# Second products of a fused attention and feed-forward block: parts of 256 and 320 columns instead of 288 and 288

## The chip, the core and the metric

The kernel runs on one core of a Trainium2 chip. The metric is the device time of one execution in microseconds (us). It was 1181.57 us before the change, the median of 3 runs from 1181.06 to 1181.97 us.

## What is computed

The input is x, 2048 rows of 576 numbers. Each row is normalised; from the normalised rows come two branches, and both are added to x:

```python
def _A_ref(x, wqkv, wo):                      # 32 heads of 18, W = 8, dil = 2
    qkv = (x @ wqkv).reshape(B, S, 3, H, Dh)...
    logits = einsum("bhsd,bhswd->bhsw", q, kg) * scale   # keys at s, s-2, ... s-14
    o = einsum("bhsw,bhswd->bhsd", softmax(masked logits), vg)
    return o @ wo
def _B_ref(x, w1, w2):                        # 576 -> 4608 -> 576
    return maximum(x @ w1, 0) @ w2
xn = _layernorm(x)
return x + _A_ref(xn, A_wqkv, A_wo) + _B_ref(xn, B_w1, B_w2)
```

All data are 32-bit floats.

## The kernel before

[...] A product is then the sum of three: high by high, high by low, low by high. The 576 rows of a contraction make four tiles of 128 and one of 64; with the 64-row rests packed in pairs, a product over 576 rows takes 14 matmuls (the list TERMS), and one over 128 rows takes three.

The 2048 rows are worked in two phases of 1024 (even and odd rows, so that the attention's step of two becomes a step of one). A phase has eight tiles of 128 rows, X[ph, i], which hold x first and collect all sums. The hidden width of 4608 is cut into 36 blocks of 128, twelve chunks (c) of three (f). The main loop runs over 288 slots: for each phase, chunk, block of 256 rows (tb, four of them) and f.

In a slot n the loop does, in this order, h_mm(n + 2), the tasks listed for the slot, and o_mm(n):

- h_mm makes the **first products**: 14 matmuls of 128 rows by 256 columns into one PSUM tile named ph. ScalarE writes the high part of the positive values (hhi, line 500), VectorE the rest (hlo, line 503).
- Tasks are the products with wqkv (14 matmuls of 432 columns into a tile named pm, in qkv_tile), loads and splits of weights, transposes, and wo_b. Attention itself runs on VectorE in a background queue that is drained according to two estimated clocks, t["pe"] and t["dve"]; mm() charges the first by the number of columns it is told.
- o_mm makes the **second products**. For each of the two 128-row tiles (k) there is a PSUM tile named po of two banks, 512 numbers a partition each. The stationary operand is a block of hhi or hlo, the moving one a half of a 128 x 576 block of w2 (w2t), high or low. For each of the three terms j there are two matmuls, h = 0 and h = 1, one for each half of 576 columns; each goes to the start of its own bank. So a slot has 12 such matmuls, in which the halves alternate. Sums are kept in PSUM over the three f of a chunk, and after f = 2 o_out adds them to X on VectorE (line 544, one instruction for both halves). There are two po tiles in all, one for each k.
- wo_b multiplies one tile of the attention's result by wo: 14 terms, two matmuls of 288 columns each, into two pm tiles, added to X by two instructions (line 466). This occurs 16 times.

The last slot is treated apart. Its matmuls are sorted by half, so that the first half is complete sooner, and each half is added (line 550) and sent to the output on its own (line 551), from two queues.

All matmuls but the transposes have line 105, the helper mm. TensorE loads the stationary operand anew for each matmul (PEld in the profile).

Of the kernel before, what the change touches and what calls it, by code (L numbers as in the profile page):

```python
# [10 lines left out]
F32 = mybir.dt.float32  # L11
F32R = mybir.dt.float32r
AF = mybir.ActivationFunctionType
ALU = mybir.AluOpType
# [3 lines left out]
P = 128  # L18
# [29 lines left out]
def tile_body(ctx: ExitStack, tc: tile.TileContext, x, wqkv, wo, w1, w2, out):  # L48
    nc = tc.nc
    S, D = x.shape  # L50
# [5 lines left out]
    KT = 4  # L56
    DR = D - KT * P
    D2 = D // 2
    scale = Dh ** -0.5
    SPC = NTB * C  # L60
    SPP = NCH * SPC
# [21 lines left out]
    ps_m = pool("ps_m", 2, space=PSUM)  # L83
# [15 lines left out]
    o_v = out.rearrange("(p i two) d -> two i p d", i=NI, two=NPH)  # L99
# [4 lines left out]
    def mm(o, l, r, start, stop, n):  # L104
        nc.tensor.matmul(o, l, r, start=start, stop=stop)  # L105
        t["pe"] += n / 2400.0 + 0.002

    def dve(n):
        t["dve"] += (n + 130) / 960.0
# [111 lines left out]
    X, XT, XN, MR = {}, {}, {}, {}  # L221
# [7 lines left out]
    def stats(ph, i, parts=False):  # L229
# [7 lines left out]
        def sums():  # L237
            for h in range(2):
                nc.vector.bn_stats(st[:, h, :], xt[:, h * D2 : (h + 1) * D2])  # L239

# [66 lines left out]
    TERMS = [(k, k) for k in range(KT)] + [(5 + k, k) for k in range(KT)] + [(4, 4)] + [(k, 5 + k) for k in range(5)]  # L307
# [149 lines left out]

    def wo_b(ph, i):
        d, w = OT.pop((ph, i)), WO[ph]
        po = [ps_m.tile([P, D2], F32, name="pm") for _ in range(2)]  # L460
        for j, (a, b) in enumerate(TERMS):
            for h in range(2):
                mm(po[h], d[a], w[b][:, h * D2 : (h + 1) * D2], j == 0, j == len(TERMS) - 1, D2)
        for h in range(2):
            acc = X[ph, i][:, h * D2 : (h + 1) * D2]
            nc.vector.tensor_tensor(acc, po[h], acc, op=ALU.add)
            dve(D2)

    left = {(ph, i): 2 for ph in range(NPH) for i in range(NI)}

    def done(ph, i):
        left[ph, i] -= 1
        if left[ph, i] == 0:
            nc.sync.dma_start(o_v[ph, i], X[ph, i])
# [3 lines left out]
    H, PO = {}, {}  # L478
# [14 lines left out]
    def h_out(n, parts=False):  # L493
        pt = HP.pop(n)
        hi = hp.tile([P, TBN], F32R, name="hhi")
        lo = hp.tile([P, TBN], F32R, name="hlo")
        H[n] = (hi, lo)

        def high():
            nc.scalar.activation(hi, pt, AF.Relu)  # L500

        def low():
            nc.vector.scalar_tensor_tensor(lo, pt, 0.0, f32(hi), op0=ALU.max, op1=ALU.subtract)  # L503
            t["dve"] = max(t["dve"], t["pe"] + 0.6)
            dve(TBN)

        if not parts:
            high()
            low()
        return high, low  # L510

    def h_mm(n):
        h_terms(n, TERMS)
        h_out(n)

    def o_mm(n, out=True):
        ph, c, tb, f = slots[n]
        hi, lo = H.pop(n)
        w = W2[ph, c, f]
        end = n == len(slots) - 1  # L520
        for k in range(2):
            if f == 0:
                PO[k] = ps_o.tile([P, 2, 512], F32, name="po")
            cs = slice(k * P, (k + 1) * P)
            terms = [(j, l, b, h) for j, (l, b) in enumerate(((hi, 0), (hi, 1), (lo, 0))) for h in range(2)]
            if end:
                terms.sort(key=lambda z: z[3])
            for j, l, b, h in terms:
                mm(
                    PO[k][:, h, 0:D2], l[:, cs], w[:, b, h * D2 : (h + 1) * D2],  # L530
                    f == 0 and j == 0, f == C - 1 and j == 2, D2,
                )
        if out:
            o_out(n)

    def o_out(n, which=range(2)):
        ph, c, tb, f = slots[n]
        if f < C - 1:
            return
        for k in which:  # L540
            i = 2 * tb + k
            acc = X[ph, i].rearrange("p (h c) -> p h c", h=2)
            if n < len(slots) - 1:
                nc.vector.tensor_tensor(acc, PO[k][:, :, 0:D2], acc, op=ALU.add)  # L544
                dve(D)
                if c == NCH - 1:
                    done(ph, i)
                continue
            for h in range(2):
                nc.vector.tensor_tensor(acc[:, h], PO[k][:, h, 0:D2], acc[:, h], op=ALU.add)  # L550
                (nc.scalar if h else nc.sync).dma_start(o_v[ph, i][:, h * D2 : (h + 1) * D2], acc[:, h])
            left[ph, i] -= 1
            assert left[ph, i] == 0

# [12 lines left out]
    for ph in range(NPH):  # L567
        b = ph * SPP
# [14 lines left out]
        for i in range(NI):  # L583
            z = s + WO_STEPS[i]
            late(z, wo_a, ph, i)
            at(z + 1, wo_f, ph, i)
            late(z + 2, wo_s, ph, i)
            at(z + 3, wo_b, ph, i)
            at(z + 3, done, ph, i)
# [63 lines left out]
    x2[1]()  # L653
    x2[3]()
    o_mm(0)
    o_mm(1)
    make_xt(0, 3, bank=ps_h)
    o_mm(2, out=False)
    stats(0, 4)
    stats(0, 5)  # L660
# [4 lines left out]
    h4 = h_out(4, parts=True)  # L665
    h4[0]()
    o_out(2, (0,))
    make_xt(0, 4)
    o_out(2, (1,))
    h4[1]()  # L670
    h_terms(5, TERMS)
# [47 lines left out]
```

## Time and profile before

| | us |
|---|---|
| Median of 3 runs (lowest, highest) | 1181.57 (1181.06, 1181.97) |
| The profiled execution | 1181.42 |
| Its span, from first to last instruction | 1179.7 |
| TensorE busy | 1171.0 |
| VectorE busy | 818.8 |
| ScalarE busy | 301.9 |

The span is what the profile sees of the execution; 1.7 us lie around it. TensorE's busy time is that of matmuls which overlap one another, so that a single one's duration is not its price. A row of the timeline has the start in us, the length in us, the engine, the line, the operation, the tiles written and read, the shape and the count of instructions merged into it; a row of the groups has the total busy time and the mean duration in ns of one instruction, and then the idle time before the group with what ended it.

### The profile page before, as it was taken

To read this page: it belongs to the slowest core of one execution; us is meant where nothing else is said; L and a number is where in the kernel's file an instruction comes from. 1 tells how busy PE (TensorE), PEld (TensorE's weight loads), DVE (VectorE), ACT (ScalarE), POOL (GpSimd) and SP (SyncE) were. 2 spreads that over 40 slices of the span, in tenths; PEclk is the share of its full clock that TensorE was granted. 3 is DMA by queue.
4 is the path that set the end of the run, shared out by engine and by line. 5 is a ranking of instruction groups with operands and counts; after the bars stand their busy time and mean duration, and the time that the engine had idled before them with its cause. 6 is when DMAs were issued, how large, how long until landed. Compare 5 with 4: busy or idle time off the path is not lost.

```text
span 1179.7 us, 21695 instructions
## 1 busy us (share of the span) xinstructions
PE 1171.0 (99%) x8936; PEld 1162.3 (99%) x8936; DVE 818.8 (69%) x1298; ACT 301.9 (26%) x738; POOL 47.5 (4%) x70
## 2 busy tenths in 40 slices
PE   8999999999999999999999999999999999999998
PEld 8999999999999999999999999999999999999998
DVE  7427875888687678877673288758777884887752
ACT  5412222131222222321233123121222322222210
POOL 3200000010000000000020000000100000000000
PEclk9999999999999999999999999999999999999999
DMA  5312121130321211355342113030302313113431
GB/s 182 97 34 76 55 61 56 38 108 1 99 58 46 74 48 42 94 129 134 107 148 66 46 53 88 27 83 23 96 22 79 79 34 89 54 30 99 110 99 61
DMA packets 137650, 86.15 MB, mean 73 GB/s; under 512 B 48864, under 2 KB 121312, under 8 KB 137552
## 3 DMA queue, kind: packets, MB, share of 16 engines
q1 hardware_dynamic: 134736, 76.28, 23.7%
q10 hardware_dynamic: 2816, 8.49, 2.5%
q8 instruction: 70, 1.15, 0.4%
q14 instruction: 28, 0.23, 0.1%
HBM read 66.58 MB, written 9.96 MB: 65 GB/s over the span
## 4 chain that ended last, share of the span: by engine, by line
PE 96%; DVE 1%; DMA 1%; ACT 0%; issue 0%; POOL 0%; SPq 0%; DVEq 0%; ACTq 0%; POOLq 0%
PE ph L105 38%; PE po L105 38%; PE pm L105 20%; PE pm L274 0%; DVE bst L239 0%; DMA xn<-turned 0%; DMA x<-in_x 0%; DMA st<-in_wqkv 0%; DMA turned<-tr 0%; DVE pr L395 0%; POOL rstd L245 0%; DVE w2t L141 0%; ACT xn L257 0%; DVE hlo L503 0%; DVE x L550 0%
## 5 line engine op out<-in xcount | busy, mean ns | idle before, releaser
L105 PE MATMUL ph<-xT,w1t 128*128 128x256 f32 x4018 | 509.3, 278 | 0.7 <-ACT xT L279 0.7
L105 PEld LDWEIGHTS ph<-xT,w1t 128*128 128x128 f32 x4018 | 489.1, 188 | 1.1 <-ACT xT L279 1.0
L105 PE MATMUL po<-w2t,hhi 128*128 128x288 f32 x2304 | 400.7, 296 | 0.0
L105 PEld LDWEIGHTS po<-w2t,hhi 128*128 128x128 f32 x2304 | 337.0, 188 | 1.0
L500 ACT ACTIVATE hhi<-ph 128x256 fp32r<-128x256 f32 x287 | 109.9, 383 | 583.4 <-PE ph L105 560.2
L105 PE MATMUL po<-w2t,hlo 128*128 128x288 f32 x1152 | 245.0, 293 | 0.0
L503 DVE SCALAR_TENSOR_TENSOR hlo<-ph,hhi 128x256 fp32r<-128x256 f32 x287 | 120.8, 421 | 169.2 <-ACT hhi L500 168.5
L544 DVE TENSOR_TENSOR x<-po,x 128x576 f32<-128x576 f32 x190 | 142.5, 756 | 67.2 <-PE po L105 64.1
L105 PE MATMUL pm<-wq,xT 128*128 128x432 f32 x896 | 185.5, 358 | 0.0
L105 PEld LDWEIGHTS po<-w2t,hlo 128*128 128x128 f32 x1152 | 183.8, 188 | 0.0
L105 PEld LDWEIGHTS pm<-wq,xT 128*128 128x128 f32 x896 | 163.8, 188 | 5.6
L358 DVE TENSOR_TENSOR pr<-qo,k 128x1152 f32<-128x1152 f32 x64 | 85.8, 1348 | 0.0
L361 DVE TENSOR_REDUCE lg<-pr 128x64 f32<-128x1152 f32 x64 | 84.9, 1342 | 0.0
L388 DVE TENSOR_TENSOR pr<-lg,v 128x1152 f32<-128x1152 f32 x64 | 84.6, 1348 | 0.2
L141 DVE TENSOR_TENSOR w2t<-st,w2t 128x576 fp32r<-128x576 f32 x72 | 54.3, 754 | 40.4 <-ACT w2t L137 40.2
L395 DVE TENSOR_TENSOR pr<-pr 128x288 f32<-128x288 f32 (+1 forms) x128 | 70.4, 598 | 0.1
L141 DVE TENSOR_TENSOR w1t<-st,w1t 128x640 fp32r<-128x640 f32 x70 | 57.3, 818 | 12.1 <-ACT w1t L137 12.0
L137 ACT ACTIVATE w2t<-st 128x576 fp32r<-128x576 f32 x72 | 49.3, 685 | 55.1 <-PE po L105 46.5
L327 ACT ACTIVATE k<-pm 128x144 f32<-128x144 f32 x64 | 18.6, 291 | 146.5 <-PE pm L105 146.5
L137 ACT ACTIVATE w1t<-st 128x640 fp32r<-128x640 f32 x72 | 52.9, 735 | 2.5 <-DMA st<-in_w 2.3
L364 POOL TENSOR_SCALAR_AFFINE_SELECT lg<-lg 1x512 f32<-1x512 f32 x8 | 9.4, 1172 | 836.7 <-DVE lg L361 836.7
L105 PE MATMUL pm<-wq,oT 128*128 128x288 f32 x224 | 35.2, 296 | 0.8 <-ACT oT L451 0.8
(71 smaller groups left out, 444.2 us busy)
## 6 DMA issues: line engine op xcount, KB each, us to landing
st<-in_w SPq DMA_DIRECT2D x72, 288.0 KB, 3.0
st<-in_w SPq DMA_DIRECT2D x72, 256.0 KB, 3.1
st<-in_wqkv SPq DMA_DIRECT2D x32, 216.0 KB, 3.1
turned<-tr SPq DMA_DIRECT2D x64, 80.0 KB, 2.2
xn<-turned SPq DMA_DIRECT2D x16, 320.0 KB, 3.3
st<-in_w SPq DMA_DIRECT2D x144, 32.0 KB, 2.8
x<-in_x SPq DMA_DIRECT2D x15, 288.0 KB, 4.4
out<-x SPq DMA_DIRECT2D x14, 288.0 KB, 2.2
```

Of the source, the lines that this page charges most:

```text
L105: nc.tensor.matmul(o, l, r, start=start, stop=stop)
L137: nc.scalar.activation(hi, src, AF.Copy)
L141: nc.vector.tensor_tensor(lo, src, f32(hi), op=ALU.subtract)
L327: nc.scalar.activation(k[:, W - 1 + i, :], pq[:, 1, :], AF.Copy)
L358: nc.vector.tensor_tensor(pr[i], q, window(k, i), op=ALU.mult)
L361: nc.vector.tensor_reduce(lg[:, i], pr.pop(i).rearrange(heads, d=Dh), axis=AX.X, op=ALU.add)
L364: nc.gpsimd.affine_select(out=z, in_=z, pattern=[[1, NI], [1, W], [0, HG]], compare_op=ALU.is_ge, fill=-1e9 / scale, base=1 - W, channel_m ...
L388: nc.vector.tensor_tensor(pr[i].rearrange(heads, d=Dh), e, window(v, i).rearrange(heads, d=Dh), op=ALU.mult)
L395: nc.vector.tensor_tensor(o, z[:, 0:n], z[:, n : 2 * n], op=ALU.add)
L500: nc.scalar.activation(hi, pt, AF.Relu)
L503: nc.vector.scalar_tensor_tensor(lo, pt, 0.0, f32(hi), op0=ALU.max, op1=ALU.subtract)
L544: nc.vector.tensor_tensor(acc, PO[k][:, :, 0:D2], acc, op=ALU.add)
```

## The change

The 576 columns are cut at 256 instead of at 288, in the second products and in those with wo. In a po tile the first part now takes the second half of the first bank (columns 256 to 511) and the second part the first 320 columns of the second bank, so that the two lie side by side over the border between the banks. The addition to X after a chunk reads them as one run of 576 columns instead of two runs of 288. In wo_b the two pm tiles have 256 and 320 columns. In the last slot the two additions and the two transfers to the output have 256 and 320 columns. mm() is told 288 columns (D2) for either part, as before.

```diff
+    CUT = (slice(0, 256), slice(256, D))
...
     def wo_b(ph, i):
         d, w = OT.pop((ph, i)), WO[ph]
-        po = [ps_m.tile([P, D2], F32, name="pm") for _ in range(2)]
+        po = [ps_m.tile([P, c.stop - c.start], F32, name="pm") for c in CUT]
         for j, (a, b) in enumerate(TERMS):
-            for h in range(2):
-                mm(po[h], d[a], w[b][:, h * D2 : (h + 1) * D2], j == 0, j == len(TERMS) - 1, D2)
-        for h in range(2):
-            acc = X[ph, i][:, h * D2 : (h + 1) * D2]
+            for h, c in enumerate(CUT):
+                mm(po[h], d[a], w[b][:, c], j == 0, j == len(TERMS) - 1, D2)
+        for h, c in enumerate(CUT):
+            acc = X[ph, i][:, c]
             nc.vector.tensor_tensor(acc, po[h], acc, op=ALU.add)
             dve(D2)
...
+    def half(po, h):
+        return po[:, 1, 0 : D - 256] if h else po[:, 0, 256:512]
...
                 mm(
-                    PO[k][:, h, 0:D2], l[:, cs], w[:, b, h * D2 : (h + 1) * D2],
+                    half(PO[k], h), l[:, cs], w[:, b, CUT[h]],
                     f == 0 and j == 0, f == C - 1 and j == 2, D2,
                 )
...
-            acc = X[ph, i].rearrange("p (h c) -> p h c", h=2)
+            acc = X[ph, i]
             if n < len(slots) - 1:
-                nc.vector.tensor_tensor(acc, PO[k][:, :, 0:D2], acc, op=ALU.add)
+                whole = PO[k].rearrange("p b c -> p (b c)")[:, 256 : 256 + D]
+                nc.vector.tensor_tensor(acc, whole, acc, op=ALU.add)
                 dve(D)
                 if c == NCH - 1:
                     done(ph, i)
                 continue
-            for h in range(2):
-                nc.vector.tensor_tensor(acc[:, h], PO[k][:, h, 0:D2], acc[:, h], op=ALU.add)
-                (nc.scalar if h else nc.sync).dma_start(o_v[ph, i][:, h * D2 : (h + 1) * D2], acc[:, h])
+            for h, c in enumerate(CUT):
+                nc.vector.tensor_tensor(acc[:, c], half(PO[k], h), acc[:, c], op=ALU.add)
+                (nc.scalar if h else nc.sync).dma_start(o_v[ph, i][:, c], acc[:, c])
```

## The prediction

> **What bounds the kernel now.** I read the busy shares first, then the chain of waits, then TensorE's waits, then the groups, then the timeline of TensorE alone.
>
> ```profile
> span 1179.7 us, 21695 instructions
> PE 1171.0 (99%) x8936; PEld 1162.3 (99%) x8936; DVE 818.8 (69%) x1298; ACT 301.9 (26%) x738; POOL 47.5 (4%) x70
> PE 96%; DVE 1%; DMA 1%; ACT 0%; issue 0%; POOL 0%; SPq 0%; DVEq 0%; ACTq 0%; POOLq 0%
> PE ph L105 38%; PE po L105 38%; PE pm L105 20%; PE pm L274 0%; DVE bst L239 0%; DMA xn<-turned 0%; DMA x<-in_x 0%; DMA st<-in_wqkv 0%; DMA turned<-tr 0%; DVE pr L395 0%; POOL rstd L245 0%; DVE w2t L141 0%; ACT xn L257 0%; DVE hlo L503 0%; DVE x L550 0%
> ```
>
> The chain that ended last is TensorE for 96% of the span: first products (ph), second products (po) and the rest (pm). Nothing else holds it up.
>
> ```profile
> PE po L96 <- POOL mhalf L90: 1.4, 1, 1.4
> PE pm L105 <- ACT oT L451: 0.8, 1, 0.8
> PE po L274 <- DVE xn L260: 0.8, 1, 0.8
> PE ph L105 <- ACT xT L279: 0.7, 1, 0.7
> ```
>
> These are the largest waits of TensorE, us in total first; all its waits together are under 6 us, most of them at the start. So the time is the sum of the distances between matmul starts, and only what alters that distance counts. The groups give the forms:
>
> ```profile
> L105 PE MATMUL ph<-xT,w1t 128*128 128x256 f32 x4018 | 509.3, 278 | 0.7 <-ACT xT L279 0.7
> L105 PE MATMUL po<-w2t,hhi 128*128 128x288 f32 x2304 | 400.7, 296 | 0.0
> L544 DVE TENSOR_TENSOR x<-po,x 128x576 f32<-128x576 f32 x190 | 142.5, 756 | 67.2 <-PE po L105 64.1
> ```
>
> Their means (278 and 296 ns) can't be used: matmuls overlap, and a mean holds the depth of the pipeline. The price of a matmul is the distance to the next start. The timeline of TensorE shows it, each row a run of matmuls with its start:
>
> ```profile
> 12.82 1.82 PE L105 MATMUL pm<-xT,w1t 128*128 128x256 f32 x14
> 14.47 0.60 PE L274 MATMUL pm<-ident,xn 128*128 128x128 f32 x4
> ...
> 28.20 1.78 PE L105 MATMUL ph<-xT,w1t 128*128 128x256 f32 x14
> 29.81 0.69 PE L105 MATMUL po<-w2t,hhi 128*128 128x288 f32 x4
> 30.34 0.42 PE L105 MATMUL po<-w2t,hlo 128*128 128x288 f32 x2
> 30.60 0.70 PE L105 MATMUL po<-w2t,hhi 128*128 128x288 f32 x4
> 31.14 0.42 PE L105 MATMUL po<-w2t,hlo 128*128 128x288 f32 x2
> 31.40 1.78 PE L105 MATMUL ph<-xT,w1t 128*128 128x256 f32 x14
> ...
> 64.92 2.90 PE L105 MATMUL pm<-wq,xT 128*128 128x432 f32 x14
> 67.66 0.70 PE L105 MATMUL po<-w2t,hhi 128*128 128x288 f32 x4
> ```
>
> From start to start: 14 matmuls of 256 columns take 29.81 - 28.20 = 1.61 us, 115 ns each; 12 of 288 take 31.40 - 29.81 = 1.59 us, 132.5 ns each; 14 of 432 take 2.74 us, 195.7 ns each. Over the whole trace the mean distance after a matmul is 115.7 ns for ph (4018), 132.5 ns for po (3455), and 195.5 ns for the 432-column ones (896). The mean granted clock of the run is 1.0, so none of this is a throttled clock.
>
> Three things are to be seen in the single starts. From 288 to 432 columns a column costs (195.5 - 132.5) / 144 = 0.4375 ns. That line gives 118.5 ns at 256 columns, and the 14 matmuls at 12.82 us do run at 1.65 / 14 = 117.9 ns. But in nearly all other groups of first products only the first five distances lie there (means 120.1, 116.6, 117.2, 120.2, 117.2 ns); the next eight stand at 113.3 ns, dead regular. Thus 256 columns have two gaits, **unsettled** at about 118 ns, on the line of the other widths, and **settled** at 113.3 ns; groups of 288 show 131 to 133 ns with single ones of 140, and never a lasting fast gait but for 18 matmuls from 15.80 to 18.15 us at 130.6 ns.
>
> **The change, part by part.** *Counts.* No instruction is added or removed. The 3456 second products become 1728 narrow (256) and 1728 wide (320), alternating; those with wo, 16 tiles x 14 terms, become 224 of each. That makes 1952 pairs. The planner's clock is still charged 288 columns for either, so order, loads and background work stay as they are. No step, queue or DMA is moved and no wait is added.
>
> *A pair.* Now 2 x 132.5 = 265.0 ns (the wo groups, 3.72 us for 28 on the chain, lie within 1 ns of that). Neither an alternation nor 320 columns occur in the trace, so both halves are bounded. Narrow: from 113.3 ns (settled) to 120.1 ns (the first ph matmul after a po matmul, the nearest place to a narrow one that follows a wide one). I take 115.7, the mean of all first products, which holds both gaits. Wide: from 113.3 x 320 / 256 = 141.6 ns (settled at the same ns per column) to 132.5 x 320 / 288 = 147.2 ns; I take 146.5, the line through 288 and 432 carried to 320, since two measured widths lie on it. The pair is then 262.2 ns, 2.8 ns less, and 1952 x 2.8 = 5.5 us off the path. The ends: 254.9 ns (19.7 us less) and 267.3 ns (4.5 us more).
>
> *What the pairs hand to the first products.* Each ph group starts with five unsettled distances, 24.8 ns over five settled ones. After a wide matmul instead of a 288 one this may go to nothing (288 groups x 24.8 ns = 7.1 us less) or spread over the whole group (117.9 - 115.7 = 2.2 ns on 4018 matmuls, 8.8 us more). I take 0, the start after po groups of one kind being the only row.
>
> *The additions to x.* The 190 of L544 read 576 columns of PSUM in one run over the border instead of two runs of 288. The nearest rows are 756 ns for the two runs and 754 ns for the same operation on 576 unbroken columns in SBUF; I take 0, with 0.1 us either way as bound for one of them. VectorE waits 64.1 us for po before them, and TensorE covers them: after a chunk's last slot it does a ph group (1.61 us) before it writes a po tile again, and the second tile half a po group (0.8 us) after that, while the two additions take 1.5 us; without that cover 190 x the difference would count. The 32 additions of the wo products change from twice 288 to 256 + 320, the same sum.
>
> *The end.* The last tile's additions (452 ns for 288 columns) become 256 and 320. At (756 - 452) / 288 = 1.06 ns a column the last one is 34 ns longer, the half before it 34 shorter; the last transfer grows by a ninth. The last six matmuls of each tile still hold three of either width. I put 0.05 us, between 0 and 0.1.
>
> *Sum.* The profiled execution took 1181.42 us, 1179.7 of it span and 1.7 around it. Less 5.5, plus 0.05: 1175.9; against the median of 1181.57, which is 0.15 above it, about **1176 us**, a gain of 0.5%. What can be told from no change in this kernel is some 0.2%, 2.4 us.
>
> A rule speaks against a gain. The Trainium skill's page "TensorE: Matmul & The Clock Gate", section "Back-to-back issue gap", has a warm matmul cost its columns / 2.4 plus about 2.5 ns; then 109.2 + 135.8 is exactly twice 122.5, and nothing changes. The trace disagrees with its sizes (115.7, 132.5 and 195.5 where it has 109.2, 122.5 and 182.5).
>
> **The rivals.**
>
> *Columns cost the same wherever they stand.* On the line through 288 and 432 the pair is 118.5 + 146.5 = 265.0 ns, the present one to the tenth, and the time stays at 1181.6 us. For it: the 14 at 12.82 us and the first five of each group lie on this line, and a gait that needs five equal matmuls to set in may never do so in pairs. Against it: a fast gait exists in most 256-column matmuls. The cited rule would end here too. Chance 0.14.
>
> *Both widths settle.* At 254.9 ns a pair the time is 1181.6 - 19.7 = 1161.9 us, and 1155 if the first products also settle at once. For it: 320 is 256 and a quarter more, 288 and 432 are not whole multiples of 64 columns, and the settled gait might hang on that. Against it: the 14 at 12.82 us have 256 columns and do not settle. Chance 0.16, with 1158 to 1170 as its share.
>
> *The settled gait is lost, and the kernel is slower.* One mechanism: every change of width upsets the gait, and the pairs change width at each matmul. The narrow one then costs what the first after a po group costs, 120.1 ns, the wide one 147.2: 267.3 ns, 1186.1 us. Handed on, the first products stay at 117.9 ns for all 14, a further 8.8 us: 1194.9. It decides as soon as a pair exceeds 265 ns by 1.3 ns, or as ph loses 0.6 ns a matmul (2.4 us each). For it: the ph groups that follow a po group begin slow, for three to five matmuls. Against it: 12 po matmuls cost 1586 or 1587 ns whether ph or the 432-column ones came before, so a change of width need not cost there. Chance 0.33; as its time I put 1188.
>
> **How the numbers follow.** My forecast, narrow ones gaining a part and ph unchanged, has 0.37 and reaches from 1170 to 1179. Faster by over 0.2%: 0.37 + 0.16 = 0.53; within: 0.14; slower: 0.33. The range, 1163 to 1190 us, takes in most of each rival and leaves out the fully settled end (about 0.07) and the end with every ph group unsettled (about 0.1).
>
> **What would show it.** In the changed kernel's TensorE timeline, a po group of 12 should last 1.57 us instead of 1.59, and a ph group 1.61. Single starts after a narrow matmul should be near 116 ns, after a wide one near 146. If the po group lasts 1.59 the line holds; at 1.53 both widths settle; at 1.60 and with ph at 1.65 the gait is lost. L544 should still be near 756 ns and hold up nothing. The prediction is wrong if a po group and a ph group together, now 3.20 us, do not fall below 3.195.

## The result, and the profile after

The changed kernel takes 1170.62 us, the median of 5 runs (1169.80 to 1171.44); the kernel before took 1181.57 us (5 runs). The ratio is 0.9907, 95% interval 0.9896 to 0.9917: 11.0 us or 0.93% less. The profiled execution took 1169.8 us, 11.6 less than that of before.

The page of the changed kernel, its span, its busy shares, its chain and the groups that answer to those shown of before:

```profile
span 1168.0 us, 21695 instructions
PE 1159.1 (99%) x8936; PEld 1150.1 (98%) x8936; DVE 817.3 (70%) x1298; ACT 301.6 (26%) x738; POOL 47.6 (4%) x70
PE 95%; DVE 2%; DMA 1%; ACT 1%; issue 0%; SPq 0%; POOL 0%; DVEq 0%; ACTq 0%; POOLq 0%
L106 PE MATMUL ph<-xT,w1t 128*128 128x256 f32 x4018 | 504.7, 277 | 0.7 <-ACT xT L280 0.7
L106 PE MATMUL po<-w2t,hhi 128*128 128x256 f32 (+1 forms) x2304 | 395.7, 293 | 0.0
L549 DVE TENSOR_TENSOR x<-po,x 128x576 f32<-128x576 f32 x190 | 142.3, 756 | 66.0 <-PE po L106 64.2
```

The instructions are as many as before, and TensorE still holds 95% of the chain (96% before). The addition over the bank border (line 549) takes 756 ns as the one in two runs did. So the gain lies in the distances between matmul starts, and the timeline of TensorE shows it (in these rows the 256 columns are those of the first of the merged matmuls; every second one has 320):

```profile
86.84 1.76 PE L106 MATMUL ph<-xT,w1t 128*128 128x256 f32 x14
88.43 0.68 PE L106 MATMUL po<-w2t,hhi 128*128 128x256 f32 x4
88.95 0.42 PE L106 MATMUL po<-w2t,hlo 128*128 128x256 f32 x2
89.21 0.68 PE L106 MATMUL po<-w2t,hhi 128*128 128x256 f32 x4
89.73 0.42 PE L106 MATMUL po<-w2t,hlo 128*128 128x256 f32 x2
89.99 1.76 PE L106 MATMUL ph<-xT,w1t 128*128 128x256 f32 x14
```

A group of second products lasts 89.99 - 88.43 = 1.56 us (before 1.59), one of first products 88.43 - 86.84 = 1.59 (before 1.61). Added up over the whole trace, each distance put to the matmul that it follows:

| | before, us (ns each) | after, us (ns each) | difference, us |
|---|---|---|---|
| second products | 457.8 (132.5) | 451.7 (120.4 narrow, 141.1 wide) | -6.1 |
| first products (ph) | 465.0 (115.7) | 460.2 (114.5) | -4.8 |
| products with wo | 60.3 (134.6) | 59.3 | -1.0 |
| products with wqkv | 175.2 (195.5) | 175.2 (195.6) | 0 |

Single distances tell how. These are the medians by place in a group, in ns, of po groups that follow ph and of ph groups that follow po:

```
po before   133 132 133 132 130 131 131 132 140 131 131 131
po after    119 140 120 140 120 140 120 140 120 140 120 140
ph before   119 117 118 122 118 113 113 113 113 113 113 113 113 113
ph after    118 116 114 113 113 113 113 113 113 113 113 113 113 113
```

The pairs have a settled gait of their own, 120 + 140 = 260 ns, as regular as the 113.3 ns of the first products; and the first products that follow it settle after three matmuls instead of five.

### The profile page after: what moved, and what is told of

Same layout as the page of the kernel before. It is cut to its first block, busy times and chain, and to the rows that moved or that the text cites. A ratio compares the mean times of both kernels' runs of the same rounds, so it can differ in the third digit from the quotient of the medians.

```text
span 1168.0 us, 21695 instructions
## 1 busy us (share of the span) xinstructions
PE 1159.1 (99%) x8936; PEld 1150.1 (98%) x8936; DVE 817.3 (70%) x1298; ACT 301.6 (26%) x738; POOL 47.6 (4%) x70
## 4 chain that ended last, share of the span: by engine, by line
PE 95%; DVE 2%; DMA 1%; ACT 1%; issue 0%; SPq 0%; POOL 0%; DVEq 0%; ACTq 0%; POOLq 0%
PE ph L106 37%; PE po L106 37%; PE pm L106 20%; DMA xn<-turned 1%; PE pm L275 0%; DVE bst L240 0%; DMA turned<-tr 0%; DVE pr L396 0%; DMA x<-in_x 0%; DVE hlo L504 0%; DVE x L549 0%; DMA st<-in_wqkv 0%; SPq L438 0%; POOL rstd L246 0%; DVE w2t L142 0%
## 5 line engine op out<-in xcount | busy, mean ns | idle before, releaser
L106 PE MATMUL po<-w2t,hhi 128*128 128x256 f32 (+1 forms) x2304 | 395.7, 293 | 0.0
L106 PE MATMUL po<-w2t,hlo 128*128 128x256 f32 (+1 forms) x1152 | 243.9, 292 | 0.0
L106 PEld LDWEIGHTS po<-w2t,hlo 128*128 128x128 f32 x1152 | 190.1, 187 | 0.0
L106 PE MATMUL pm<-wq,oT 128*128 128x256 f32 x224 | 34.6, 293 | 0.5 <-ACT oT L452 0.4
```

## The experiments

Four theories stood at first: (A) the two widths in turn make the gain; (B) the place in PSUM or the single addition makes it; (C, E) the order of the matmuls does; (A1, A2) widths that are whole multiples of 64 columns settle, or any uneven cut does. Theory F, the place in SBUF, came up later.

### The place in PSUM alone

```diff
-    CUT = (slice(0, 256), slice(256, D))
+    CUT = (slice(0, 288), slice(288, D))
...
-        return po[:, 1, 0 : D - 256] if h else po[:, 0, 256:512]
+        return po[:, 1, 0 : D - 288] if h else po[:, 0, 512 - 288 : 512]
...
```

> 288 and 288 columns as before, but side by side over the bank border and added to x as one run of 576. Theory A (the widths make the gain: a narrow and a wide matmul in turn stand at 120 + 140 ns): pairs stay at 264 to 265 ns, time 1181 to 1182 us. Rival B (the place in PSUM, or the addition in one run, makes it): pairs at 260 to 262 ns or shorter additions than 756 ns, time 1170 to 1176 us.

Measured: 1181.23 us, ratio 0.9998 (0.9988 to 1.0007); second products 457.9 us, first products 464.5, additions 757 ns. The placement over the border and the single addition are worth nothing; B falls.

### The second products alone

```diff
     def wo_b(ph, i):
+        CUT = (slice(0, D2), slice(D2, D))
```

> 256 and 320 columns for the second products alone, 288 and 288 with wo. Theory A: 1728 of the 1952 pairs and the shorter start of the first products remain; only the wo part of the trace (60.3 us before, 59.2 after) is given back, so 1171 to 1172.5 us. Rival B': the wo products carry a share well above their 11% of the pairs: 1174 us or more.

Measured: 1171.69 us, ratio 0.9918 (0.9903 to 0.9932). The products with wo are worth 1.1 us, in step with their share of the trace; the rest belongs to the second products and what follows them.

### The wide part first

```diff
-    CUT = (slice(0, 256), slice(256, D))
+    CUT = (slice(0, 320), slice(320, D))
```

(with the place in PSUM moved accordingly)

> 320 columns first, then 256. Theory A (only the two widths in turn count): pairs again at 260 ns; a group of first products now follows a narrow matmul, so its first three distances (118.2, 115.9, 114.2 ns after the change) fall to 113.3, 8.4 ns x 288 = 2.4 us, time 1167 to 1169 us. Rival C (it counts which width comes first in a group): pairs fall back toward 264 ns, 1176 us or more.

Measured: 1175.22 us, ratio 0.9948 (0.9931 to 0.9964), between the two and a miss for both. The medians:

```
po after ph     147 117 144 118 142 118 140 120 140 120 140 118
po after wqkv   151 117 147 117 153 117 147 117 153 117 147 117
ph              119 121 116 114 113 113 113 113 113 113 113 113 113 113
```

The pair of 140 + 120 exists here too, but the group needs six matmuls to find it, and behind the 432-column products it never does: there a pair takes 264 to 270 ns. So the same pair of widths has an unsettled gait as well, and which one runs depends on what came before. A first product behind a narrow matmul is no better off (119, 121), against what A expected.

### Other widths

```diff
-    CUT = (slice(0, 256), slice(256, D))
+    CUT = (slice(0, 272), slice(272, D))
```

(with the place in PSUM moved accordingly)

> 272 and 304 columns. Theory A1 (what counts is that both widths are whole multiples of 64 columns): no fast gait, pairs at 264 to 265 ns, 1180 to 1183 us. Rival A2 (any uneven cut does it, since alternation alone sets the fast gait): pairs at 260 ns, about 1171 us.

Measured: 1179.51 us, ratio 0.9983 (0.9974 to 0.9993). Pairs take 125.6 + 139.0 = 264.6 ns and circle through 127, 138, 122, 140, 127, 139, 124, 135; the 2 us come in parts of under 1 us from all three kinds of group. So not every uneven cut does it (A2 falls). That multiples of 64 columns are the reason (A1) does not follow from this. A cut also sets where the second part of w2 begins in its row of 576 four-byte numbers: at byte 1152 with 288 columns, 1024 with 256 and 1088 with 272. No run separates that place from the widths; the next one shows that byte 1024 alone does not give the gain.

### Narrow ones together, then wide ones

Both tiles' narrow matmuls come first, directly behind the first products of the same width.

```diff
-        for k in range(2):
...
+        terms = [
+            (j, l, b, h, k) for k in range(2)
+            for j, (l, b) in enumerate(((hi, 0), (hi, 1), (lo, 0))) for h in range(2)
+        ]
+        terms.sort(key=lambda z: (z[4], z[3]) if end else z[3])
+        for j, l, b, h, k in terms:
```

> 256 and 320 columns; in each slot the six narrow second products (of both po tiles) come first, right behind the first products, which have 256 columns too, then the six wide ones; wo as in the changed kernel. Theory A (each width has a settled gait, and a change of width costs some steps out of it): the narrow ones go on at 113.3 ns, the wide ones stand between 140 ns (settled) and 146.5 (the line), a group of 12 at 1520 to 1559 ns instead of 1560, time 1159 to 1170 us. Rival D (the fast gait hangs on the alternation of a narrow and a wide one): narrow ones at 118 and wide ones at 146.5 ns, 1587 ns a group, 1176 us or more.

Measured: 1180.31 us, ratio 0.9989 (0.9979 to 0.9998): 9.7 us of the 11 are gone. The medians of a group are 119 113 117 123 120 119 and then 144 146 147 147 145 147; its timeline (six rows of 256, then of 320 columns; the merged rows are by tile):

```profile
92.24 0.39 PE L106 MATMUL po<-w2t,hhi 128*128 128x256 f32 x2
92.47 0.28 PE L106 MATMUL po<-w2t,hlo 128*128 128x256 f32 x1
92.58 0.41 PE L106 MATMUL po<-w2t,hhi 128*128 128x256 f32 x2
92.83 0.28 PE L106 MATMUL po<-w2t,hlo 128*128 128x256 f32 x1
92.95 0.45 PE L106 MATMUL po<-w2t,hhi 128*128 128x320 f32 x2
...
93.82 1.76 PE L106 MATMUL ph<-xT,w1t 128*128 128x256 f32 x14
```

Six narrow ones take 0.71 us, 118 ns each, and six wide ones 0.87 us, 145 ns each. Rival D holds: here the fast gait hangs on the alternation. The width of 256 columns alone isn't what settles, for six of them behind fourteen others of that width did not.

The control for the order, the same with 288 and 288:

> The same order of the matmuls as in the grouped kernel, but with 288 and 288 columns: the control for the order. Theory A: the order alone does nothing, groups of 12 stay at 1586 ns, 1180 to 1183 us. Rival E (the order, which spreads the matmuls into one PSUM bank differently, gives the gain): 1176 us or less.

Measured: 1182.84 us, ratio 1.0011 (1.0001 to 1.0020); second products 460.3 us instead of 457.8. The order alone gains nothing (1.3 us more, under the 2.4 us that the prediction takes for no change); E falls.

### A wider product with wqkv, and what it brought to light

```diff
-                    WQ[key] = wqp.tile([P, 10, 3 * UD], F32R, name="wq")
+                    WQ[key] = wqp.tile([P, 10, 448], F32R, name="wq")
...
-        pq = ps_m.tile([P, 3, UD], F32, name="pm")
+        pw = ps_m.tile([P, 448], F32, name="pm")
+        pq = pw[:, 0 : 3 * UD].rearrange("p (s c) -> p s c", s=3)
...
```

> The changed kernel, in which the matmuls with wqkv have 448 columns instead of 432: 16 columns of a constant are appended to wqkv's tile and their products are never read. Theory A1 (whole multiples of 64 columns settle into a faster gait): 193.3 ns or less each instead of 195.5 despite 16 more columns, 896 x 2.2 = 2 us or more less, 1166 to 1169 us. Rival B (columns cost the same wherever they stand, and 256 with 320 is a case of its own): 195.5 + 16 x 0.4375 = 202.5 ns, 6.3 us more, 1177 us.

Measured: 1198.89 us, ratio 1.0146 (1.0131 to 1.0162): far outside both expectations. The wider products themselves cost only 4.3 us more (200.4 ns each); but first products stood at 117.8 ns in the mean and pairs at 118 + 149 = 267. This was so in most groups before the first wqkv product was issued at 41 us. Until then the one difference to TensorE's operands is a side effect: the larger tile pushes everything that is allocated behind it, hhi and hlo among it, 640 bytes up in SBUF. Hence theory F, and four kernels that shift without widening.

### The place in SBUF

```diff
     wqp = pool("wqp", 1)
+    gap = pool("gap", 1).tile([P, 160], F32, name="gap")
```

> The changed kernel with 640 unused bytes a partition behind wqkv's tile, so that hhi, hlo and all that is allocated later lie 640 bytes higher, as in the kernel with 448 columns; wqkv keeps 432 columns. Theory F (the gait hangs on where the stationary blocks hhi and hlo lie in SBUF): pairs at 267 ns and first products at 117.8 ns as in that kernel, whose time less its 4.3 us for the wider matmuls is 1194 to 1195 us. Rival G (the 448 columns upset the gait): 1170 to 1172 us.

Measured: 1198.02 us, ratio 1.0142 (1.0127 to 1.0157). Nothing but the place of buffers differs from the changed kernel, whose timeline stands above:

```profile
87.89 1.81 PE L107 MATMUL ph<-xT,w1t 128*128 128x256 f32 x14
89.54 0.70 PE L107 MATMUL po<-w2t,hhi 128*128 128x256 f32 x4
90.08 0.43 PE L107 MATMUL po<-w2t,hlo 128*128 128x256 f32 x2
90.35 0.70 PE L107 MATMUL po<-w2t,hhi 128*128 128x256 f32 x4
90.88 0.43 PE L107 MATMUL po<-w2t,hlo 128*128 128x256 f32 x2
91.15 1.81 PE L107 MATMUL ph<-xT,w1t 128*128 128x256 f32 x14
```

A po group lasts 1.61 us instead of 1.56, a ph group 1.65 instead of 1.59, at the same counts and a granted clock of 1.0. G falls and F holds, as far as a shift of all these buffers can show it, though the time is 3 us above what F gave. The medians are 122 147 120 149 118 149 118 149 118 149 118 149 for po, and 117 to 119 all through for ph, whose own operands (xT and w1t) did not move. The start of this trace shows what the slow first products hang on:

```profile
12.77 1.75 PE L107 MATMUL pm<-xT,w1t 128*128 128x256 f32 x14
14.36 0.60 PE L276 MATMUL pm<-ident,xn 128*128 128x128 f32 x4
...
24.50 1.85 PE L107 MATMUL ph<-xT,w1t 128*128 128x256 f32 x14
26.18 0.60 PE L276 MATMUL pm<-ident,xn 128*128 128x128 f32 x4
```

The fourteen at 12.77 us, ahead of any second product, take 14.36 - 12.77 = 1.59 us, 113.6 ns each. The group at 24.50 us follows transposes; its first distance is 206 ns, and from the third on they are 113 to 115 ns. All three groups of first products that follow transposes end at 113 to 114 ns; of the 282 that follow second products, one does. So at this place the slow gait comes to the first products from what runs before them.

The kernel before the change, with the same 640 bytes:

> The kernel before the change with the same 640 unused bytes. Theory F: the distances of 288-column matmuls and the unsettled part of the first products change too; with first products at 117.9 ns throughout some 1190 us, and at least 2.4 us away from 1181.5. Rival G: 1181 to 1182 us.

Measured: 1192.73 us, ratio 1.0096 (1.0081 to 1.0111). The 288-column groups hardly change in sum (458.9 us for 457.8), and the products with wqkv take 1.5 us more (176.7 for 175.2). Most of the loss lies in the first products: 473.6 us for 465.0, 117.9 ns each in the mean. Behind second products 250 of 282 groups don't settle; 32 do, among them all in the first 39 us and those from 521 to 634 us. A group that doesn't:

```profile
91.08 1.81 PE L106 MATMUL ph<-xT,w1t 128*128 128x256 f32 x14
92.73 0.70 PE L106 MATMUL po<-w2t,hhi 128*128 128x288 f32 x4
93.27 0.42 PE L106 MATMUL po<-w2t,hlo 128*128 128x288 f32 x2
93.53 0.69 PE L106 MATMUL po<-w2t,hhi 128*128 128x288 f32 x4
94.06 0.42 PE L106 MATMUL po<-w2t,hlo 128*128 128x288 f32 x2
94.32 1.81 PE L106 MATMUL ph<-xT,w1t 128*128 128x256 f32 x14
```

Set against each other at this place, 1198.0 and 1192.7 us, the change makes the kernel 5.3 us **slower**.

Two more shifts of the changed kernel, by 512 and by 384 bytes:

> The changed kernel with 512 unused bytes in the same place. Theory F with a period of 512 bytes (the two halves of hhi lie 512 bytes apart and keep the same gait): 1170 to 1172 us. Theory F without such a period: 1174 us or more. Rival G: 1170 to 1172 us, and then the kernels with 640 bytes too.

Measured: 1170.68 us, ratio 0.9910 (0.9893 to 0.9926), with the medians of po behind ph, and of ph behind po, as in the changed kernel.

> The changed kernel with 384 unused bytes, which puts hhi and hlo on whole multiples of 512 bytes. Theory F: a gait of its own, away from 1170.6 us by more than 2.4 us, to either side (1163 to 1195 us). Rival G: 1170 to 1172 us.

Measured: 1197.82 us, ratio 1.0139 (1.0123 to 1.0154), 3 us beyond the stated range; the medians are those with 640 bytes, within 1 ns.

The last run shifts by 768 bytes in all and tries the 448 columns again:

> The changed kernel with 448 columns for wqkv again (640 bytes, columns of a constant whose products are never read) and 128 unused bytes more, so that hhi and hlo lie 768 bytes higher than in the changed kernel. Theory F with a period of 256 bytes (offsets 128 and 640 from a multiple of 1024 gave the fast gait, 0, 256, 512 and 768 the slow one): pairs at 260 ns and settled first products from the start on, and then the 448-column matmuls are read undisturbed: 193.3 ns and 1168 to 1169 us if whole multiples of 64 columns settle (A1), 200 to 202.5 ns and 1175 to 1177 us if they do not. Theory F with a period of 512 bytes and the fast gait at 128 alone: pairs at 264 to 267 ns, 1185 to 1200 us.

Measured: 1173.78 us, ratio 0.9935 (0.9918 to 0.9952). Pairs are back at 260 ns and ph at 114.7:

```profile
86.96 1.76 PE L107 MATMUL ph<-xT,w1t 128*128 128x256 f32 x14
88.56 0.68 PE L107 MATMUL po<-w2t,hhi 128*128 128x256 f32 x4
...
90.12 1.76 PE L107 MATMUL ph<-xT,w1t 128*128 128x256 f32 x14
```

The 448-column matmuls go round 197, 202, 201 ns, 200.2 in the mean; the time is 1 us under the range given for that. They don't settle, so a whole multiple of 64 columns is not enough (A1 falls). Put together, with the distance of hhi and hlo above a multiple of 256 bytes as the build allots them (192640 for the first hhi in the changed kernel):

| bytes added | offset in 256 | regular pair, ns | first products, mean ns | time, us |
|---|---|---|---|---|
| 0 | 128 | 260 | 114.5 | 1170.62 |
| 512 | 128 | 260 | 114.7 | 1170.68 |
| 768, with 448 columns | 128 | 260 | 114.7 | 1173.78 |
| 384 | 0 | 267 | 118.2 | 1197.82 |
| 640 | 0 | 267 | 118.2 | 1198.02 |
| 640, with 448 columns | 0 | 267 | 117.8 | 1198.89 |

Time follows the offset in 256 bytes: 27 us lie between its two values, 25 with 448 columns. No other offset was tried, and what is moved is not hhi and hlo alone but all that is allocated behind them too (staged weights, x normalised, the attention's buffers; not xT, w1t and w2t). In the changed kernel with 640 bytes, pairs of 118 + 149 ns stand from the first group of second products on (14.82 us), and the first slow group of first products is the first behind second products (20.47 us). Second products read only hhi, hlo and the unmoved w2t, first products nothing that moved. That points to hhi and hlo; moving them alone was not tried, and in the kernel of before the sum of the second products hardly changes. Nor does the offset fix every group: behind second products, 34 of 282 groups of first products settle with 448 columns at offset 0, and 32 in the shifted kernel of before.

## Why the prediction was right, and where it was not

The frame held. The time is the sum of matmul distances, the additions and the end are worth nothing that can be seen, nothing waits anew, and the time fell, within the range. The size was half of the measured one: 5.5 us against 11.0. That the time fell at all was in part luck: it hung on where hhi and hlo happen to lie, which the prediction did not consider, and 640 bytes higher the same change costs 5.3 us.

**The pair.** Forecast 262.2 ns; measured 261.5 in the mean for the second products and 260 settled. The total is near by luck, for both halves were mis-sized, by 4.7 and 5.4 ns in opposite directions. The narrow one was taken at 115.7 from the mean of the first products and came to 120.4. The nearest row by its surroundings, the first matmul behind a wider one, had 120.1, and this upper end of the bound was the right one. The wide one was taken from the line at 146.5 and came to 141.1, settled 140, just under the lower end of 141.6. In the grouped kernel, where the widths don't alternate, the wide ones did take 146.1 in the mean. Second products and wo together gave 7.1 us by the trace where 5.5 was forecast.

**What the pairs hand on.** This was set at 0, with 7.1 us less as one end. It is worth 4.8 us, most of what was missing: the first products settle two matmuls sooner. Seeing that groups influence one another was right; putting the term at nothing, between two opposite ends, was the weak step. At this place 4.8 us are gained, two thirds of the way to one end, and with 640 bytes added the first products take 474.8 us, 9.8 more than before the change, which is past the other end (8.8).

**The rivals.** The line with no change (0.14) did not come: the pair is 3.5 ns below 265. "Both widths settle" came half: neither 113.3 nor 141.6, but a joint gait. The slower rival was wrong for the kernel as it stands and near in its sizes at another place: at 256-byte offset 0 the pairs cost 267 ns (it said 267.3), and first products stay at 118.2 ns (it said 117.9). Its time, 1186 to 1195 us, is close to the 1198 us of that placement. Its mechanism, that a change of width upsets the gait, is not what the runs show: alternation also carries the fast gait, and with 640 bytes the kernel of before loses most of its fast first products with the same widths as ever.

**The cited rule.** By the formula in the Trainium skill's page "TensorE: Matmul & The Clock Gate", section "Back-to-back issue gap", two cuts of the same columns cost the same. The page gives this formula for an isolated matmul, and says that in a stream of loads and matmuls, as here, both set the spacing. The runs show 260 to 270 ns for one and the same pair, by its surroundings. The same page, section "Step-by-step: what each phase is for", says that loading the next stationary block takes no read bandwidth from the running matmul. The kernels shifted by 384 and 640 bytes sit ill with that: buffers were moved, instructions were not, and matmuls run 2 to 3% slower. They don't show that the load is the cause, though.

## What to carry to other kernels

When TensorE never waits, look at distances between single starts, not at mean durations: a form may have two gaits, here 3 to 4% apart, and which one runs may depend on the group before it. Before judging a cut or a width, run it at two or three placements in SBUF, since a gain of 0.9% at one offset was a loss of 0.4% at another. And a change that enlarges a buffer moves all that lies behind it; a control that moves without enlarging costs one line.

## What was not expected

A shift of 384 or 640 bytes, with no instruction changed, costs 27 us (2.3%) in the changed kernel, while 512 bytes cost nothing; 640 bytes cost 11 us (1.0%) in the kernel before. The settled distances are 113.3, 120 and 140 ns, which are 17, 18 and 21 times 6.67 ns. Single distances of the slow gaits fit no such grid, but their cycles do: three first products (118.3, 117.5, 117.5) take 353.3 ns, a slow pair (117.5 and 149.2) 266.7, three of 448 columns (197, 202, 201) 600.0, which are 53, 40 and 90 times 6.67. Where such a step would come from, and why 256 and 320 columns find the fast cycle at one offset and not at the other, stays open. So does whether yet another offset would beat the changed kernel; none of the runs did.
